# Chunked attention, SoLU and leaky MLP on one core: the scores of a tile taken three tiles ahead, behind the values' product

## The chip, the cores and the metric

The kernel runs on one core of a Trainium2 chip. The metric is the device time of one execution in microseconds (us), lower is better. The median over three runs is compared; besides, one execution was profiled, and every duration below is from that one.

## What is computed

```
# q, k, v: (8, 8, 576, 64); heads cut into chunks of 64 positions
scores = scale * q_c @ k_c.T ; scores -= max(scores)
attn   = exp(scores) / (sum(exp(scores)) + 1e-9)
x      = (attn @ v_c), heads laid side by side   # (4608, 512)

h    = x @ w_in                                  # (4608, 1024)
solu = h * softmax(h)
ln   = (solu - mean) / sqrt(var + 1e-6) * g_ln
y    = ln @ w_out                                # (4608, 512)

h2  = y @ w_in2 ; g = max(0.01 * h2, h2)         # (4608, 2048)
out = g @ w_out2                                 # (4608, 512)
```

The weights arrive as 64-bit floats and are made 32-bit on the chip. The large products are taken in split form (a high part and a remainder), three matmuls for one.

## The kernel before

The 4608 rows are 36 tiles of 128 (`T = 36`). The program has a first part, up to about 560 us, in which the loop `for t in range(T + 2)` (L506) makes attention, the first product, SoLU, the norm and the second product, and a second part (L622, L665) with the last two products. The change is in the first part alone. Everything stands in an order written out by hand, under `manual_schedule`: each engine gets its instructions in the order in which the Python code records them, and waits where an input is not there yet.

One tile goes through the loop in a staggered way. In iteration t, these steps are recorded (names as in the code, then what the trace calls the results):

- `qk_mm` (L287, `s_ps`): the scores of tile t+2, 8 small matmuls into one PSUM bank. Its inputs `qt` and `kbd` come by `load_qk`, from SyncE's queue.
- `solu_a(t-1)`: on VectorE (DVE) the maximum of h, 1024 wide (L374, `z`), then on ScalarE (ACT) the exponential of h (L376, `us`).
- `softmax_a(t+2)`: on DVE the maximum of the scores (L298, `st`) and a subtraction (L300, `es`), then the exponential on ACT (L303, `es`).
- `take_magnitudes` (L93), `convert` (L101 to L109, DVE) and `finish` (L116, L117 or L167 on ACT, L118 or L168 on GpSimd (POOL), for `w_in2` also L164 and L165 on DVE): pieces of the weights. Two pieces at once in iterations 0, 1 and 6 to 11, one in the others up to 33.
- `ff1_mm(t, 0)` and `ff1_mm(t, 1)` (L359, `h_ps`): the first product, two halves of 12 matmuls. The first half needs `xs` of tile t.
- `solu_b(t-1)` (L381, `us`): on DVE the product of h and its exponential. It needs the result of L376.
- `pt_mm`, `pt_copy` (L320, L326, `pt`), `softmax_b(t+2)` (L307 to L310), `pv_mm(t+1)` (L337, `x_ps`): the transposed weights of the attention and the values' product, in 64x64 pieces.
- `x_split(t+1)`: a copy on ACT (L348) and a subtraction on DVE (L349), both `xs`.
- `lnT_mm(t-2)`, `lnT_split` (L414, L420 on ACT, L421 on DVE, `lnT`), and `y1_group` (L430, `y_ps`, 24 matmuls), copied out by ACT (L438, `ys`).

From iteration 5 on there is a y group in each iteration. In every fourth (5, 9, 13, ...; `late`) the y group stands behind the values' product and needs the `lnT` of tile t-2, in the others ahead of it. Up to iteration 4 there is none, and TensorE has the scores right behind the values' product there already, since nothing else stands at the end of an iteration.

Of the kernel before, what the change touches and what calls it, by code (L numbers as in the profile page):

```python
# [23 lines left out]
T = NT // P  # L24
# [19 lines left out]
def kernel(  # L44
# [22 lines left out]
    def bank(tag, name):  # L67
        return (ps2 if tag == "ef" else ps1).tile([P, 512], F32, tag=tag, name=name)
# [113 lines left out]
    def take_magnitudes(n=1):  # L182
        for _ in range(min(n, len(loaded))):
            end, raw = loaded.pop(0)
            begun.append((end, raw, magnitudes(raw)))
# [18 lines left out]
    def y_load(g):  # L204
        if g < NG:
            for name, r, c in (("a11", 0, 0), ("a21", 1, 0), ("a22", 1, 1), ("a12", 0, 1)):
                yr[name] = yp.tile([P, 2, TH], F32, tag=name, name=name)
                sync.dma_start(
                    out=yr[name], in_=y_d[g][:, 2 * c : 2 * c + 2, r * TH : (r + 1) * TH]
                )  # L210
# [31 lines left out]
    def w_load():  # L242
        at = next(w_order, None)
        if at:
            w = ws.tile([P, 2, 2 * P], F32R, tag="w", name="w_s")
            sync.dma_start(out=w.bitcast(F32), in_=wi_d[at[0]][:, w_place[at[1]]])
            w_tiles.append(w)

    wf_bufs = None
    with tc.manual_schedule():  # L250

        with ExitStack() as phase:
# [12 lines left out]
            def load_qk(t):  # L265
                if t >= T:
                    return
                qt[t] = pa.tile([P, KD, P], F32, tag="qt", name="qt")
                sync.dma_start(out=qt[t], in_=q[t])
                kb = kbd[t % 2]  # L270
                for e in range(2):
                    sync.dma_start(out=kb[e * D : (e + 1) * D, e], in_=k[t, e * D : (e + 1) * D])

            def load_v(t):
                if t >= T:
                    return
                vt[t] = pa.tile([P, KD, 2, D], F32, tag="vt", name="vt")
                sync.dma_start(out=vt[t], in_=v[t])
# [3 lines left out]
            def qk_mm(t):  # L282
                ps = s_ps[t] = bank("ef" if t in (1, 2) else "s", "s_ps").rearrange("p (h n) -> p h n", h=H)
                kb, qq = kbd[t % 2], qt.pop(t)
                for i in range(KD):
                    for c in range(2):
                        pe.matmul(  # L287
                            ps[c * D : (c + 1) * D, 2 * i : 2 * i + 2, :],
                            lhsT=qq[:, i, c * D : (c + 1) * D],
                            rhs=kb[:, :, i, c, :],  # L290
                            start=True,
                            stop=True,
                        )

            def softmax_a(t):
                ps = s_ps.pop(t)
                sm = st8[t] = pa.tile([P, 2, H], F32, tag="st8", name="st8")
                dve.reduce_max(sm[:, 0, :], ps, axis=AX)  # L298
                e = es[t] = pa.tile([P, H, D], F32, tag="es", name="es")
                dve.tensor_tensor(  # L300
                    e, ps, sm[:, 0, :].unsqueeze(2).to_broadcast([P, H, D]), op=ALU.subtract
                )
                act.activation(e, e, AF.Exp, scale=scale)  # L303
# [26 lines left out]
            def pv_mm(t):  # L330
                ps = x_ps[t] = bank("ptx", "x_ps").rearrange("p (i n) -> p i n", i=KD)
                vv, pp = vt.pop(t), pt.pop(t)
                for i in range(KD):
                    for c in range(2):
                        for e in range(2):
                            r = slice(e * D, (e + 1) * D)
                            pe.matmul(  # L337
                                ps[r, i, c * D : (c + 1) * D],
                                lhsT=vv[r, i, c, :],
                                rhs=pp[r, i, c * D : (c + 1) * D],  # L340
                                start=True,
                                stop=True,
                            )

            def x_split(t):
                ps = x_ps.pop(t)
                x = xs[t] = pa.tile([P, 2, KD, P], F32R, tag="xs", name="xs")
                act.activation(x[:, 0], ps, AF.Copy)  # L348
                dve.tensor_tensor(x[:, 1], ps, x[:, 0].bitcast(F32), op=ALU.subtract)  # L349
# [21 lines left out]
            def solu_a(t):  # L371
                h = hs[t].rearrange("p n f -> p (n f)")
                z = sol[t] = wk.tile([P, 8], F32, tag="z", bufs=3, name="z")
                dve.reduce_max(z[:, 0:1], h, axis=AX, negate=True)  # L374
                u = us[t] = wk.tile([P, FF1], F32, tag="us", bufs=3, name="us")
                act.activation(u, h, AF.Exp, bias=z[:, 0:1], accum_out=z[:, 1:2])  # L376
# [46 lines left out]
            def y1_group(b, m):  # L423
# [21 lines left out]
                g, o = divmod(pair, 3)  # L445
                sync.dma_start(out=y_d[g][:, m, o * 256 : o * 256 + 512 - at], in_=ys[:, at:])


            start = ExitStack()
            stage = start.enter_context(tc.tile_pool(name="start", bufs=5))  # L450
# [55 lines left out]
            for t in range(T + 2):  # L506
                if t == T:
                    att.close()
                    yp = ctx.enter_context(
                        tc.tile_pool(name="yp", bufs=1, side="right", reuse_waits="tile")  # L510
                    )
                    ws = ctx.enter_context(
                        tc.tile_pool(name="ws", bufs=WS, side="right", reuse_waits="tile")
                    )
                    y_load(0)
                    for _ in range(WS):
                        w_load()
                load_qk(t + 3)
                load_v(t + 2)
                b, g = divmod(t - 5, 4)  # L520
                groups = [(b, g)] if 5 <= t < T else []
                if t == T - 1:
                    groups = []
                elif t == T:
                    groups = [(NB - 2, 2), (NB - 2, 3)]
                elif t == T + 1:
                    groups = [(NB - 1, m) for m in range(KD)]
                late = g == 0 or t == T - 1
                pieces = 0 if t >= T - 2 else 2 if t < 2 or 6 <= t < 12 else 1
                if 0 < t < T - 2:  # L530
                    qk_mm(t + 2)
                if 1 <= t <= T:
                    solu_a(t - 1)
                if t + 2 < T:
                    softmax_a(t + 2)
                take_magnitudes(pieces)
                if t < T:
                    ff1_mm(t, 0)
                if 1 <= t <= T:
                    solu_b(t - 1)  # L540
                if t + 1 < T:
                    pt_mm(t + 1)
                if t + 2 < T:
                    softmax_b(t + 2)
                convert(pieces)
                if t + 1 < T:
                    pt_copy(t + 1)
                if late and t >= 2:
                    lnT_mm(t - 2)
                    lnT_split(t - 2, 0)  # L550
                    lnT_split(t - 2, 1)
                if 1 <= t <= T:
                    solu_c(t - 1)
                    solu_d(t - 1)
                if t == T:
                    for _, do in Y_STEPS:
                        do(0)
                if groups and not late:
                    for bm in groups:
                        y1_group(*bm)  # L560
                    if t + 1 < T:
                        pv_mm(t + 1)
                        x_split(t + 1)
                    if t >= 2:
                        lnT_mm(t - 2)
                        lnT_split(t - 2, 0)
                        lnT_split(t - 2, 1)
                    if t < T:
                        ff1_mm(t, 1)
                    finish(pieces)  # L570
                else:
                    if t >= 2 and not late:
                        lnT_mm(t - 2)
                        lnT_split(t - 2, 0)
                        lnT_split(t - 2, 1)
                    if t < T:
                        ff1_mm(t, 1)
                    if t + 1 < T:
                        pv_mm(t + 1)
                        x_split(t + 1)  # L580
                    finish(pieces)
                    for bm in groups:
                        y1_group(*bm)
# [171 lines left out]
```

## Time and profile before

| what | value |
|---|---|
| median of three runs (lowest, highest) | 1338.85 us (1338.63, 1339.13) |
| profiled execution, whole | 1339.17 us |
| its span from first to last instruction | 1337.4 us |
| TensorE (PE) busy | 1292.0 us, 97% |
| DVE, ACT, POOL busy | 608.4, 530.0, 448.1 us |
| mean granted TensorE clock | 0.994 |

Busy time is counted over the whole span. The engines other than TensorE are much busier in the first 230 us than later, so the shares say little on a single stage; the rows below are taken by stage.

### The profile page before, as it was taken

The numbers are of one execution on the slowest core, as the hardware profiler recorded it, in microseconds if no ns is written. First come the engines' busy times: TensorE is split into PE (matmuls) and PEld (weight loads), VectorE is DVE, ScalarE is ACT, GpSimd is POOL, SyncE is SP. The second block draws the span as 40 slices with busy tenths as digits, with TensorE's granted clock in tenths as the row PEclk, the third lists the DMA queues.
The fourth block names the chain that finished last, engine by engine and source line by source line (L and its number), as shares of the span: only waits on it lengthen the run. The fifth ranks groups of instructions, "written<-read, shape, count | busy, mean of one in ns | idle before, by whom it ended". The sixth has DMA issues, their size and how long they took to land.

```text
span 1337.4 us, 20370 instructions
## 1 busy us (share of the span) xinstructions
PE 1292.0 (97%) x7632; PEld 1116.0 (83%) x7632; DVE 608.4 (45%) x1030; ACT 530.0 (40%) x953; POOL 448.1 (34%) x488
## 2 busy tenths in 40 slices
PE   3799999999999999899999999999999999999998
PEld 3678788788888888689989998999899989989997
DVE  7988887766666654511232233222412331232112
ACT  3665554444444443423333324333332333333322
POOL 3556765433433431212222222222222222222222
PEclk9999999999999999899999999999999999999999
DMA  7345776544444432257645544554554455445441
GB/s 244 116 130 190 255 245 195 173 163 136 144 141 156 128 103 73 102 212 229 196 134 165 166 118 129 150 170 119 159 163 121 118 165 165 119 117 166 118 118 48
DMA packets 100608, 202.66 MB, mean 152 GB/s; under 512 B 10784, under 2 KB 28192, under 8 KB 98080
## 3 DMA queue, kind: packets, MB, share of 16 engines
q1 hardware_dynamic: 100512, 201.37, 49.1%
q8 instruction: 61, 1.00, 0.3%
q14 instruction: 35, 0.29, 0.1%
HBM read 159.39 MB, written 41.94 MB: 151 GB/s over the span
## 4 chain that ended last, share of the span: by engine, by line
PE 86%; DVE 8%; ACT 2%; DMA 1%; issue 1%; SPq 0%; POOL 0%; ACTq 0%; DVEq 0%
PE o_ps L665 28%; PE h_ps L622 25%; PE y_ps L430 14%; PE h_ps L359 12%; PE x_ps L337 2%; PE s_ps L287 2%; PE ln_ps L414 2%; PE pt_ps L320 1%; DVE yo L228 1%; DVE wf L109 1%; DVE wf L105 1%; ACT yo L227 1%; DVE wf L103 1%; DMA raw<-in_w_in 1%; DVE us L381 1%
## 5 line engine op out<-in xcount | busy, mean ns | idle before, releaser
L665 PE MATMUL o_ps<-wo_s,g 128*128 128x512 f32 x1728 | 447.4, 390 | 0.0
L622 PE MATMUL h_ps<-yo,w_s 128*128 128x384 f32 x2016 | 407.4, 337 | 3.0 <-DVE c L633 3.0
L604 POOL TENSOR_TENSOR g<-t,g 128x384 fp32r<-128x384 f32 x192 | 194.7, 1014 | 583.0 <-ACT g L603 496.8
L622 PEld LDWEIGHTS h_ps<-yo,w_s 128*128 128x128 f32 x2016 | 362.4, 188 | 32.8 <-DVE c L633 5.1
L665 PEld LDWEIGHTS o_ps<-wo_s,g 128*128 128x128 f32 x1728 | 319.9, 188 | 41.7
L359 PE MATMUL h_ps<-wi,xs 128*128 128x512 f32 x864 | 220.3, 403 | 2.7 <-DVE xs L349 2.7
L430 PE MATMUL y_ps<-lnT,wo 128*128 128x512 f32 x864 | 208.6, 398 | 6.5 <-DVE lnT L421 6.5
L430 PEld LDWEIGHTS y_ps<-lnT,wo 128*128 128x128 f32 x864 | 162.4, 191 | 40.9 <-DVE lnT L421 4.7
L633 DVE TENSOR_TENSOR u<-h_ps,p 128x384 f32<-128x384 f32 x96 | 53.5, 557 | 312.3 <-PE h_ps L622 304.4
L359 PEld LDWEIGHTS h_ps<-wi,xs 128*128 128x128 f32 x864 | 158.5, 190 | 41.5 <-issue 6.0
L601 ACT ACTIVATE t<-c 128x384 f32<-128x384 f32 x144 | 75.7, 526 | 286.8 <-DVE c L633 286.7
L633 DVE TENSOR_TENSOR c<-h_ps,u 128x384 f32<-128x384 f32 x96 | 53.5, 557 | 125.1 <-PE h_ps L622 73.0
L603 ACT ACTIVATE g<-t 128x384 fp32r<-128x384 f32 x192 | 100.8, 525 | 6.0
L310 POOL TENSOR_TENSOR es<-es,st 128x512 f32<-128x512 f32 x36 | 37.6, 1046 | 179.9 <-DVE st L309 152.5
L601 ACT ACTIVATE t<-h_ps 128x384 f32<-128x384 f32 x48 | 23.6, 492 | 186.8 <-PE h_ps L622 186.8
L438 ACT ACTIVATE ys<-y_ps 128x512 f32<-128x512 f32 x36 | 21.4, 596 | 133.7 <-PE y_ps L430 133.6
L376 ACT ACTIVATE us<-h_ps,z 128x1024 f32<-128x1024 f32 x36 | 40.1, 1115 | 55.8 <-DVE z L374 55.7
L349 DVE TENSOR_TENSOR xs<-x_ps,xs 128x512 fp32r<-128x512 f32 x36 | 24.8, 688 | 74.3 <-ACT xs L348 74.3
L633 DVE TENSOR_TENSOR c<-h_ps,p 128x384 f32<-128x384 f32 x48 | 26.7, 556 | 66.4 <-PE h_ps L622 66.4
L374 DVE TENSOR_REDUCE z<-h_ps 128x1 f32<-128x1024 f32 x36 | 43.8, 1217 | 22.2 <-PE h_ps L359 22.2
L287 PE MATMUL s_ps<-kbd,qt 128*64 128x128 f32 x576 | 42.0, 291 | 10.5 <-DMA kbd<-in_k 10.4
L287 PEld LDWEIGHTS s_ps<-kbd,qt 128*64 128x64 f32 x576 | 33.0, 144 | 21.3 <-issue 20.6
(68 smaller groups left out, 1138.8 us busy)
## 6 DMA issues: line engine op xcount, KB each, us to landing
w_s<-wi_d SPq DMA_DIRECT2D x336, 256.0 KB, 2.7
wi_d<-wi SPq DMA_DIRECT2D x8, 1792.0 KB, 6.7
raw<-in_w_out SPq DMA_DIRECT2D x24, 512.0 KB, 4.1
raw<-in_w_in SPq DMA_DIRECT2D x18, 512.0 KB, 6.0
qt<-in_q SPq DMA_DIRECT2D x36, 256.0 KB, 4.9
kbd<-in_k SPq DMA_DIRECT2D x72, 128.0 KB, 4.9
vt<-in_v SPq DMA_DIRECT2D x36, 256.0 KB, 4.2
a<-y_d SPq DMA_DIRECT2D x24, 384.0 KB, 5.8
```

The lines of the kernel that those rows point to most:

```text
L287: pe.matmul(ps[c * D : (c + 1) * D, 2 * i : 2 * i + 2, :], lhsT=qq[:, i, c * D : (c + 1) * D], rhs=kb[:, :, i, c, :], start=True, stop=True,)
L310: pool.tensor_tensor(e, e, sm[:, 1, :].unsqueeze(2).to_broadcast([P, H, D]), op=ALU.mult)
L359: pe.matmul(h[:, n, :], lhsT=x[:, a, kk, :], rhs=w[:, b, kk % 2, n, :], start=(kk == 0 and a == 0 and b == 0), stop=(kk == KD - 1 and a == 1),
L374: dve.reduce_max(z[:, 0:1], h, axis=AX, negate=True)
L376: act.activation(u, h, AF.Exp, bias=z[:, 0:1], accum_out=z[:, 1:2])
L430: pe.matmul(ps, lhsT=w[:, a, kk % 4, m * P : (m + 1) * P], rhs=lnT[:, c, kk, pairs, :], start=(kk == 0 and a == 0 and c == 0), stop=(kk == ...
L601: act.activation(t, src, AF.Prelu, alpha=0.01)
L603: act.activation(g[:, 0], t, AF.Copy)
L604: pool.tensor_tensor(g[:, 1], t, g[:, 0].bitcast(F32), op=ALU.subtract)
L622: pe.matmul(ps, lhsT=w[:, a, kk * P : (kk + 1) * P], rhs=y[:, c, kk, :], start=(first and kk == 0 and a == 0 and c == 0), stop=(kk == 1 an ...
L633: dve.tensor_tensor(o, ps, x, op=ALU.add)
L665: pe.matmul(ps, lhsT=x[:, a, i * P : (i + 1) * P], rhs=wos[j][:, h, c, :], start=(j == 0 and h == 0 and a == 0 and c == 0), stop=(j == QUA ...
```

## The change

The scores of a tile are recorded one iteration earlier: `qk_mm(t + 3)` directly behind `pv_mm(t + 1)`, and `softmax_a(t + 3)` directly behind `x_split(t + 1)`. `load_qk` moves to the same place and reaches one tile further. The number of instructions and the buffers stay as they are.

```diff
+            def attend(t):
+                pv_mm(t + 1)
+                if t + 3 < T:
+                    qk_mm(t + 3)
+                    load_qk(t + 4)
+                x_split(t + 1)
+                if t + 3 < T:
+                    softmax_a(t + 3)
...
-                load_qk(t + 3)
+                if t == 0:
+                    load_qk(3)
                 load_v(t + 2)
...
-                if 0 < t < T - 2:
-                    qk_mm(t + 2)
                 if 1 <= t <= T:
                     solu_a(t - 1)
-                if t + 2 < T:
-                    softmax_a(t + 2)
+                if t == 0:
+                    softmax_a(2)
...
                     if t + 1 < T:
-                        pv_mm(t + 1)
-                        x_split(t + 1)
+                        attend(t)
```

The last hunk stands twice, once in each branch of the order of the y group.

On TensorE, an iteration with the y group ahead (from the values' product on) reads before:

```order
L337 MATMUL x_ps<-pt,vt 64x64 x16
L414 MATMUL ln_ps<-ident,us 128x128 x8
L359 MATMUL h_ps<-wi_244,xs 128x512 x12
L287 MATMUL s_ps<-kbd_107,qt 64x128 x8
L359 MATMUL h_ps<-wi_180,xs 128x512 x12
L320 MATMUL pt_ps<-ident,es 128x128 x4
L430 MATMUL y_ps<-lnT,wo_355 128x512 x12
```

and of the change:

```order
L337 MATMUL x_ps<-pt,vt 64x64 x16
L287 MATMUL s_ps<-kbd_107,qt 64x128 x8
L414 MATMUL ln_ps<-ident,us 128x128 x8
L359 MATMUL h_ps<-wi_244,xs 128x512 x12
L359 MATMUL h_ps<-wi_180,xs 128x512 x12
L320 MATMUL pt_ps<-ident,es 128x128 x4
L430 MATMUL y_ps<-lnT,wo_373 128x512 x12
```

The 8 matmuls of the scores have moved from between the two halves of the first product to behind the values' product; the halves now stand side by side.

On ACT, one of the iterations 2 to 4 (with one piece of `w_out1`, L116 and L117) reads before, from the copy of `lnT` on:

```order
L420 ACTIVATE lnT<-ln_ps 128x4x128 x2
L348 ACTIVATE xs<-x_ps 128x512
L116 ACTIVATE wf<-wf,g_sb 128x512
L117 ACTIVATE wo_588<-wf 128x512
L376 ACTIVATE us,z<-h_ps,z 128x1024
L303 ACTIVATE es<-es 128x512
L93 ACTIVATE wf<-raw 128x512
```

and of the change:

```order
L420 ACTIVATE lnT<-ln_ps 128x4x128 x2
L348 ACTIVATE xs<-x_ps 128x512
L303 ACTIVATE es<-es 128x512
L116 ACTIVATE wf<-wf,g_sb 128x512
L117 ACTIVATE wo_606<-wf 128x512
L376 ACTIVATE us,z<-h_ps,z 128x1024
L93 ACTIVATE wf<-raw 128x512
```

The exponential of the scores (L303) has moved from behind that of h (L376) to ahead of the two weight copies. On DVE, an iteration from 6 on whose y group stands ahead, and in which a pair of `w_in2` pieces is finished, reads before:

```order
L349 TENSOR_TENSOR xs<-x_ps,xs 128x512
L421 TENSOR_TENSOR lnT<-ln_ps,lnT 128x4x128 x2
L164 TENSOR_TENSOR wc<-wf,wc 128x256
L165 TENSOR_TENSOR wc<-wf,wc 128x256
L374 TENSOR_REDUCE z<-h_ps 128x1
L298 TENSOR_REDUCE st_1149<-s_ps 128x8
L300 TENSOR_TENSOR es<-s_ps,st_1149 128x512
L381 SCALAR_TENSOR_TENSOR us,z<-h_ps,us 128x1024
```

and of the change:

```order
L349 TENSOR_TENSOR xs<-x_ps,xs 128x512
L298 TENSOR_REDUCE st_1104<-s_ps 128x8
L300 TENSOR_TENSOR es<-s_ps,st_1104 128x512
L421 TENSOR_TENSOR lnT<-ln_ps,lnT 128x4x128 x2
L164 TENSOR_TENSOR wc<-wf,wc 128x256
L165 TENSOR_TENSOR wc<-wf,wc 128x256
L374 TENSOR_REDUCE z<-h_ps 128x1
L381 SCALAR_TENSOR_TENSOR us,z<-h_ps,us 128x1024
```

The two steps on the scores have left the place between the maximum of h (L374) and the product that needs the exponential of h (L381). In iterations up to 4 the same two rows move from there to directly behind L349, with nothing between them and L374.

## Rows read from the trace of the kernel before

**Rows 1.** The page, busy us of each engine, share of the span, instructions.

```profile
PE 1292.0 (97%) x7632; PEld 1116.0 (83%) x7632; DVE 608.4 (45%) x1030; ACT 530.0 (40%) x953; POOL 448.1 (34%) x488
```

**Rows 2.** Windows, one iteration each: length, busy us of the engines, clock, DMA share, GB/s.

```profile
core 0: us, PE busy (x) PEld busy (x) DVE busy (x) ACT busy (x) POOL busy (x), PEclk, DMA share, GB/s
82.79:92.67 9.88, 9.41 (x86) 7.48 (x85) 9.61 (x19) 6.94 (x13) 5.69 (x8) 1.00 0.43 134
...
153.18:173.68 20.50, 18.33 (x113) 14.53 (x113) 16.36 (x29) 7.78 (x13) 14.54 (x16) 0.92 0.84 260
...
306.85:321.59 14.74, 14.74 (x110) 11.94 (x109) 9.79 (x18) 6.92 (x12) 5.72 (x8) 1.00 0.44 143
```

**Rows 3.** Timeline of TensorE at three places: start, duration, line, out<-in.

```profile
43.24 1.15 PE L337 MATMUL x_ps<-pt,vt 64*64 64x64 f32 x32
44.32 1.09 PE L287 MATMUL s_ps<-kbd,qt 128*64 128x128 f32 x16
...
48.22 0.60 PE L320 MATMUL pt_ps<-ident,es 128*128 128x128 f32 x4
...
323.51 3.01 PE L359 MATMUL h_ps<-wi,xs 128*128 128x512 f32 x12
326.45 1.09 PE L287 MATMUL s_ps<-kbd,qt 128*64 128x128 f32 x16
327.48 3.02 PE L359 MATMUL h_ps<-wi,xs 128*128 128x512 f32 x12
330.33 0.38 PE L320 MATMUL pt_ps<-ident,es 128*128 128x128 f32 x2
...
528.95 5.73 PE L359 MATMUL h_ps<-wi,xs 128*128 128x512 f32 x24
534.52 1.03 PE L414 MATMUL ln_ps<-ident,us 128*128 128x128 f32 x8
```

**Rows 4.** Timeline of DVE, iterations 2 and 3, from one xs to the next.

```profile
75.94 0.68 DVE L349 TENSOR_TENSOR xs<-x_ps,xs 128x512 fp32r<-128x512 f32 x1
76.54 1.21 DVE L374 TENSOR_REDUCE z<-h_ps 128x1 f32<-128x1024 f32 x1
77.67 0.68 DVE L298 TENSOR_REDUCE st<-s_ps 128x8 f32<-128x512 f32 x1
78.38 0.69 DVE L300 TENSOR_TENSOR es<-s_ps,st 128x512 f32<-128x512 f32 x1
79.03 1.23 DVE L381 SCALAR_TENSOR_TENSOR us<-h_ps,us 128x1024 f32<-128x1024 f32 x1
...
85.82 0.68 DVE L349 TENSOR_TENSOR xs<-x_ps,xs 128x512 fp32r<-128x512 f32 x1
```

**Rows 5.** Timeline of ACT; in brackets the idle time and what ended it.

```profile
50.84 0.66 ACT L93 ACTIVATE wf<-raw 128x512 f32<-128x512 f32 x1 [1.03 <-DMA raw<-in_w_out]
51.41 0.58 ACT L326 ACTIVATE pt<-pt_ps 128x512 f32<-128x512 f32 x1
...
74.86 0.72 ACT L116 ACTIVATE wf<-wf,g_sb 128x512 f32<-128x512 f32 x1 [0.16 <-DVE wf L109]
75.61 0.63 ACT L117 ACTIVATE wo<-wf 128x512 fp32r<-128x512 f32 x1
77.79 1.11 ACT L376 ACTIVATE us<-h_ps,z 128x1024 f32<-128x1024 f32 x1 [1.54 <-DVE z L374]
...
79.17 0.63 ACT L303 ACTIVATE es<-es 128x512 f32<-128x512 f32 x1 [0.18 <-DVE es L300]
```

**Rows 6.** Timeline of TensorE, the y groups of iterations 5 and 9.

```profile
95.24 5.74 PE L430 MATMUL y_ps<-lnT,wo 128*128 128x512 f32 x24 [1.42 <-DVE lnT L421]
...
156.50 6.69 PE L430 MATMUL y_ps<-lnT,wo 128*128 128x512 f32 x21 [2.17 <-DVE lnT L421]
```

**Rows 7.** Timeline of DVE, iterations 7 and 8 (two weight pieces each).

```profile
127.35 0.69 DVE L349 TENSOR_TENSOR xs<-x_ps,xs 128x512 fp32r<-128x512 f32 x1 [0.97 <-ACT xs L348]
...
133.82 1.22 DVE L381 SCALAR_TENSOR_TENSOR us<-h_ps,us 128x1024 f32<-128x1024 f32 x1
...
142.09 0.69 DVE L349 TENSOR_TENSOR xs<-x_ps,xs 128x512 fp32r<-128x512 f32 x1 [0.97 <-ACT xs L348]
```

More of the change, by code (lines that the diff above doesn't have):

```diff
@@ L578 @@
                     if t + 1 < T:
-                        pv_mm(t + 1)
-                        x_split(t + 1)
+                        attend(t)
                     finish(pieces)
```

## The prediction

> **What bounds the kernel now.** I read the page first, then the windows by iteration, then the timelines of TensorE, DVE and ACT. Over the span TensorE is busy 97% [rows 1], so whatever TensorE saves or waits shows in the time. The windows show that the first part of the loop is another case [rows 2]: in the iteration from 82.79 to 92.67 DVE is busy 9.61 of 9.88 us, and TensorE 9.41, partly stretched by waiting inside its blocks. In the iteration from 306.85 TensorE is busy all of its 14.74 us and DVE 9.79. So up to iteration 5 DVE sets the pace, later TensorE does, and in between, with two weight pieces an iteration, the two are close: DVE idles only 0.97 us ahead of its xs [rows 7]. Two y groups wait for DVE's lnT, 1.42 and 2.17 us [rows 6].
>
> **What TensorE saves.** Between the halves of the first product stand the scores. From the first half to the transposes it is 330.33 - 323.51 = 6.82 us [rows 3]. Where 24 of these matmuls stand in one run, it takes 534.52 - 528.95 = 5.57 us, and the scores take 327.48 - 326.45 = 1.03. Behind the values' product they cost no more: in iteration 0 they start there 44.32 - 43.24 = 1.08 us after it started, and take 1.09 like the others. So 6.82 - 5.57 - 1.03 = 0.22 us is saved per iteration, in the 28 iterations 5 to 32 (I take it for the late ones too, an estimate): 6.2 us if nothing waits. Below iteration 5 TensorE's order doesn't change.
>
> **What DVE loses up to iteration 5.** Before, DVE takes the maximum of h (76.54), then 1.36 us of work on the scores (77.67, 78.38), then L381 at 79.03 [rows 4]. In that gap ACT makes the exponential of h: it starts at 77.79 [rows 5], and L381 follows 1.24 us later with no idle time. The scores' work is exactly what fills the gap. In the change it stands ahead of the maximum; the gap of 1.25 us stays and is empty.
>
> ACT makes it worse. The scores' exponential (L303) now stands ahead of the copies L116 and L117, and must wait for DVE's L300. Counted from the start X of DVE's xs: L298 starts at X + 0.60, L300 ends at X + 2.0 (0.60, and 1.40 from 77.67 to 79.07, [rows 4]), L303 starts at X + 2.1 (79.07 to 79.17, [rows 5]), L116 0.54 later, L117 0.75 after that, L376 about 0.55 later at X + 3.95, and L381 at X + 5.2. Before it started at X + 3.1. So an iteration with one piece gets 2.1 us longer, and nothing else is slack: from L381 to the next xs DVE has 85.82 - 79.03 = 6.79 us of solid work. In iterations 0 and 1, two pieces put two more copies (1.3 us) ahead of L376: about 3.4, less 0.3 that such copies held L376 up before (an estimate); I take 3.1. Iterations 0 to 4: 2 x 3.1 + 3 x 2.1 = **+12.5 us** until lnT, and with it the y group of iteration 5 (95.24), comes. TensorE has no cover for that; it waits in the first product and ahead of this y. Only the scores, which now precede this y group, fill 1.0 us of the wait: -1.0.
>
> All this rests on ACT keeping its order. The trace shows it: at 50.84 ACT sits idle 1.03 us for a weight's transfer although the transposes (48.22 to 48.82) have been ready for the copy that comes next (51.41) [rows 3, 5]. The Trainium skill, "TensorE: Matmul & The Clock Gate" (engine queue depth, in the table at its head), calls the queues of ScalarE, VectorE and GpSimd strictly first in, first out; if a ready copy could pass a waiting exponential, the second rival's sum would hold instead.
>
> **Iterations 6 to 9.** From xs to L381 it is 133.82 - 127.35 = 6.47 us before, without idle time [rows 7]. After, two holes open: lnT's copies on ACT stand behind L303, so DVE waits from X + 2.0 to about X + 3.3 (0.1, L303's 0.54, one copy of 0.55 like that at 51.41, and 0.1), and the gap ahead of L381, 1.3 with nothing in it. That is 2.6; I take 2.7. What hides it is 0.97 us of idle time an iteration [rows 7]. Iteration 6 starts with TensorE ahead (DVE idles there after the long y); then the holes of 6, 7 and 8 less two idles reach the lnT of iteration 9: 3 x 2.7 - 2 x 1.0 = **+6.1**. Its y group, which waits 2.17 us already, starts so much later, and again takes the scores into its wait: -1.0. Iterations 10 to 13 go the same way: two with two pieces, one with one (some 1.7 us less to convert), and a y group at 13 that did not wait. Worked through like 6 to 9, that leaves +2.8 and, with the scores in the wait, -1.0.
>
> **From 14 to 32** DVE has room [rows 2]. 19 x 0.22 = 4.2 us are saved. In the four late ones among them lnT comes about 0.4 us after the scores end (the xs-to-L381 stretch is longer, as above): +1.8 in all.
>
> **TensorE's clock.** In the iteration with the 2.17 us wait the granted clock is 0.92 over 20.50 us [rows 2, 6]: 1.6 us lost at the lower level, 1.2 GHz. Iterations 5 and 13 now get waits of about 2.5 us, each worth 0 or 1.6. I count one, 1.6.
>
> SyncE's queue: `load_qk` is issued in the place of the values' product and has a whole iteration until its scores, as before; it moves ahead of the stores of `w_in2`, no later. I cost it at nothing; covered by an iteration of 9.9 us at least.
>
> **The sum**, against the profiled execution's 1339.17 us: 12.5 - 1.0 + 6.1 - 1.0 + 2.8 - 1.0 - 4.2 + 1.8 + 1.6 = +17.6; my chain of starts, done with the rows to two places, gives 0.3 to 0.5 less (the first matmul behind a y group is better fed), so +17.1: 1356.3. The median lies 0.3 lower: **1356 us**.
>
> **Rivals.** *Only TensorE's saving counts* (faster): if DVE and ACT had room everywhere, 6.2 us come off: 1332.6. For it speaks TensorE's 97%; against it DVE's 9.61 of 9.88. It decides once the holes on DVE are below the 0.3 us of slack in such an iteration; I find 2.1. The Trainium skill, "TensorEngine Tiling (Array Packing)", key properties, says that a change of the tiling mode drains the engine; the 64-wide products would then change mode three times an iteration instead of four, and this rival is what that rule would make of the change. The trace agrees as far as 0.22 us goes. Chance 8%. *The hole without the queue* (about no change): ACT's copies don't hold L376 up and lnT isn't late. Then 5 x 1.25 - 1.0 + 3 x 1.3 - 2 x 1.0 - 1.0 - 4.2 = +2.0: 1341. It needs ACT out of order, which 50.84 speaks against, or a slack that I overlook. Chance 10%. *The clock falls with every wait* (slower still): TensorE now waits 2.6 to 3.6 us in each of iterations 1 to 4 as well, and if the lower clock reaches DVE's chain through a late xs, up to 1.6 us come on top at three or four places: +5, 1361. Against it: after xs TensorE has about 3 us to spare before DVE needs the next. Chance 12%.
>
> **How the numbers follow.** Forecast 70%, by itself 1350 to 1360: the piece terms of iterations 6 to 13 are good to 4 us, the clock to 2. The range 1341 to 1361 takes in the second rival's time and leaves out the first, half of the second and half of the third (19%). Within 0.2% (2.7 us, about what a measurement of this kernel can tell from no change) falls most of the second rival. Faster 0.09, same 0.07, slower 0.84.
>
> **What would show it.** In the changed profile: DVE idle ahead of L381, released by ACT's L376, 1.3 to 3.3 us in iterations 1 to 4; ACT idle ahead of L303, released by DVE, with L116 behind it; TensorE waiting at L359 for DVE's xs 2.5 us and more where it was about 0.5; the y of iteration 5 near 107.7 and that of 9 near 174; the first product in runs of 24 in 5.57 us from iteration 6 on. Wrong would be: no idle time ahead of L381, or L116 ahead of L303 in time, or the y of iteration 5 below 100.

## The result, and the profile after

| | before | change |
|---|---|---|
| median (lowest to highest) | 1338.94 us (1338.63 to 1339.13) | 1357.56 us (1356.95 to 1357.75) |
| ratio, 95% interval | | 1.0139 (1.0121 to 1.0156): slower |
| span of the profiled execution | 1337.4 us | 1355.9 us |

The forecast was 1356 us. The page has TensorE 3.3 us busier, and DVE and ACT no busier at all:

```profile
PE 1295.3 (96%) x7632; PEld 1124.8 (83%) x7632; DVE 605.9 (45%) x1030; ACT 526.3 (39%) x953; POOL 449.1 (33%) x488
```

So of the 18.5 us of span, 15.2 are idle time of TensorE: it waits 8.1 us in the first product for xs (2.7 before), 11.2 at the y groups for lnT (6.5) and 5.5 ahead of the values' product (1.6). The 3.3 us of busy time are net: the y groups take 212.7 us instead of 208.6 and the first product 215.5 instead of 220.3, at a mean granted clock of 0.987 (0.994 before). The timeline of DVE from one xs to the next shows where the waits come from (in brackets the idle time and what ended it). Counted by the values' products, [rows 4] run from the xs of iteration 3 to that of iteration 4; these rows stand one iteration earlier and have the same steps:

```profile
71.15 0.69 DVE L109 SCALAR_TENSOR_TENSOR wf<-raw,wf 128x512 uint32<-128x512 uint32 x1
...
72.95 0.68 DVE L349 TENSOR_TENSOR xs<-x_ps,xs 128x512 fp32r<-128x512 f32 x1
73.55 0.68 DVE L298 TENSOR_REDUCE st<-s_ps 128x8 f32<-128x512 f32 x1
74.27 0.69 DVE L300 TENSOR_TENSOR es<-s_ps,st 128x512 f32<-128x512 f32 x1
74.88 1.22 DVE L374 TENSOR_REDUCE z<-h_ps 128x1 f32<-128x1024 f32 x1
78.08 1.23 DVE L381 SCALAR_TENSOR_TENSOR us<-h_ps,us 128x1024 f32<-128x1024 f32 x1 [1.99 <-ACT us L376]
...
84.86 0.68 DVE L349 TENSOR_TENSOR xs<-x_ps,xs 128x512 fp32r<-128x512 f32 x1
```

Between the maximum of h (L374) and the product L381 there is now a hole of 1.99 us. From xs to xs it is 84.86 - 72.95 = 11.91 us (and the same in the next iteration, the one of [rows 4]), where it was 9.88 [rows 4]; from L381 to the next xs it is 6.78, as before. ACT's timeline in the same stretch says why the hole is longer than the exponential of h:

```profile
69.74 0.59 ACT L348 ACTIVATE xs<-x_ps 128x512 fp32r<-128x512 f32 x1
75.05 0.63 ACT L303 ACTIVATE es<-es 128x512 f32<-128x512 f32 x1 [4.72 <-DVE es L300]
75.59 0.70 ACT L116 ACTIVATE wf<-wf,g_sb 128x512 f32<-128x512 f32 x1
76.33 0.63 ACT L117 ACTIVATE wo<-wf 128x512 fp32r<-128x512 f32 x1
76.86 1.10 ACT L376 ACTIVATE us<-h_ps,z 128x1024 f32<-128x1024 f32 x1
```

ACT is idle for 4.72 us ahead of the scores' exponential (L303). The two weight copies, whose input DVE had made by 71.84 (L109 above), stand behind it until 75.59, and only then comes L376. In the iterations with a pair of weight pieces, DVE shows both of the holes that were forecast there, one ahead of L421 and one ahead of L381 (against [rows 7]):

```profile
141.38 0.68 DVE L349 TENSOR_TENSOR xs<-x_ps,xs 128x512 fp32r<-128x512 f32 x1
141.98 0.68 DVE L298 TENSOR_REDUCE st<-s_ps 128x8 f32<-128x512 f32 x1
142.69 0.69 DVE L300 TENSOR_TENSOR es<-s_ps,st 128x512 f32<-128x512 f32 x1
144.56 1.29 DVE L421 TENSOR_TENSOR lnT<-ln_ps,lnT 128x512 fp32r<-128x512 f32 x2 [1.18 <-ACT lnT L420]
...
150.46 1.23 DVE L381 SCALAR_TENSOR_TENSOR us<-h_ps,us 128x1024 f32<-128x1024 f32 x1 [1.27 <-ACT us L376]
```

xs to L381 takes 9.08 us instead of 6.47. TensorE's timeline has the y groups of iterations 5, 9 and 13, the first two to be read against [rows 6]:

```profile
108.21 5.51 PE L430 MATMUL y_ps<-lnT,wo 128*128 128x512 f32 x23 [0.82 <-DVE lnT L421]
...
174.67 8.56 PE L430 MATMUL y_ps<-lnT,wo 128*128 128x512 f32 x24 [4.12 <-DVE lnT L421]
...
237.82 7.36 PE L430 MATMUL y_ps<-lnT,wo 128*128 128x512 f32 x24 [2.16 <-DVE lnT L421]
```

The third, and the values' product of iteration 34, were before at

```profile
217.15 5.75 PE L430 MATMUL y_ps<-lnT,wo 128*128 128x512 f32 x24
...
527.02 1.15 PE L337 MATMUL x_ps<-pt,vt 64*64 64x64 f32 x32
```

The y groups start 13.0 us (95.24), 18.2 us (156.50) and 20.7 us (217.15) later than before. After that the kernel wins back: the values' product of iteration 34 now starts at 544.87, 17.9 us later. What it wins on TensorE, in an iteration with the y group ahead [rows 3]:

```profile
326.91 1.15 PE L337 MATMUL x_ps<-pt,vt 64*64 64x64 f32 x32
327.99 1.09 PE L287 MATMUL s_ps<-kbd,qt 128*64 128x128 f32 x16
329.01 1.09 PE L414 MATMUL ln_ps<-ident,us 128*128 128x128 f32 x8
329.86 5.70 PE L359 MATMUL h_ps<-wi,xs 128*128 128x512 f32 x24
335.40 0.60 PE L320 MATMUL pt_ps<-ident,es 128*128 128x128 f32 x4
```

The two halves run as one in 335.40 - 329.86 = 5.54 us. The windows of one iteration each follow (length, busy us of the engines, granted clock, DMA share, GB/s), to be read against [rows 2]:

```profile
core 0: us, PE busy (x) PEld busy (x) DVE busy (x) ACT busy (x) POOL busy (x), PEclk, DMA share, GB/s
...
68.28:81.41 13.13, 11.02 (x86) 8.83 (x85) 10.76 (x23) 7.95 (x16) 6.18 (x8) 0.87 0.35 102
...
168.37:191.81 23.44, 19.32 (x112) 15.49 (x113) 17.23 (x36) 9.47 (x17) 14.47 (x16) 0.85 0.71 258
...
326.91:341.42 14.51, 14.51 (x110) 12.02 (x109) 9.82 (x18) 6.81 (x12) 5.71 (x8) 1.00 0.46 146
```

An iteration late in the loop takes 14.51 us, not 14.74. In the early ones DVE is no longer solidly busy (10.76 of 13.13 us), and the granted clock is below 1 in several.

### The profile page after: what moved, and what is told of

Same layout as the page of the kernel before. It is cut to its first block, busy times and chain, and to the rows that moved or that the text cites. A ratio compares the mean times of both kernels' runs of the same rounds, so it can differ in the third digit from the quotient of the medians.

```text
span 1355.9 us, 20337 instructions
## 1 busy us (share of the span) xinstructions
PE 1295.3 (96%) x7632; PEld 1124.8 (83%) x7632; DVE 605.9 (45%) x1030; ACT 526.3 (39%) x953; POOL 449.1 (33%) x488
## 4 chain that ended last, share of the span: by engine, by line
PE 78%; DVE 13%; ACT 4%; issue 2%; DMA 2%; POOL 0%; SPq 0%; ACTq 0%; DVEq 0%
PE o_ps L672 27%; PE h_ps L629 25%; PE y_ps L430 13%; PE h_ps L359 8%; PE x_ps L337 2%; DVE lnT L421 2%; DVE us L381 1%; PE ln_ps L414 1%; DVE wf L103 1%; DVE wf L105 1%; DVE wf L109 1%; PE s_ps L287 1%; DVE yo L228 1%; ACT us L376 1%; DMA raw<-in_w_in 1%
## 5 line engine op out<-in xcount | busy, mean ns | idle before, releaser
L430 PE MATMUL y_ps<-lnT,wo 128*128 128x512 f32 x864 | 212.7, 403 | 11.6 <-DVE lnT L421 11.2
L359 PE MATMUL h_ps<-wi,xs 128*128 128x512 f32 x864 | 215.5, 402 | 8.4 <-DVE xs L349 8.1
L359 PEld LDWEIGHTS h_ps<-wi,xs 128*128 128x128 f32 x864 | 162.0, 192 | 43.8 <-DVE xs L349 9.9
L381 DVE SCALAR_TENSOR_TENSOR us<-h_ps,us 128x1024 f32<-128x1024 f32 x36 | 44.1, 1225 | 77.5 <-ACT us L376 77.5
L303 ACT ACTIVATE es<-es 128x512 f32<-128x512 f32 x36 | 22.8, 632 | 109.4 <-DVE es L300 109.4
L118 POOL TENSOR_TENSOR wo<-wf,wo 128x512 fp32r<-128x512 f32 x24 | 30.9, 1287 | 87.0 <-ACT wo L117 87.0
L421 DVE TENSOR_TENSOR lnT<-ln_ps,lnT 128x512 fp32r<-128x512 f32 x72 | 46.1, 684 | 25.7 <-ACT lnT L420 25.7
L337 PEld LDWEIGHTS x_ps<-pt,vt 64*64 64x64 f32 x1152 | 37.2, 137 | 18.5 <-issue 10.4
```

The lines of the kernel that those rows point to most:

```text
L337: pe.matmul(ps[r, i, c * D : (c + 1) * D], lhsT=vv[r, i, c, :], rhs=pp[r, i, c * D : (c + 1) * D], start=True, stop=True,)
L359: pe.matmul(h[:, n, :], lhsT=x[:, a, kk, :], rhs=w[:, b, kk % 2, n, :], start=(kk == 0 and a == 0 and b == 0), stop=(kk == KD - 1 and a == 1),
L381: dve.scalar_tensor_tensor(u, h, 1.0, u, op0=ALU.mult, op1=ALU.mult, accum_out=z[:, 2:3])
L421: dve.tensor_tensor(dst[:, 1], ps, dst[:, 0].bitcast(F32), op=ALU.subtract)
L430: pe.matmul(ps, lhsT=w[:, a, kk % 4, m * P : (m + 1) * P], rhs=lnT[:, c, kk, pairs, :], start=(kk == 0 and a == 0 and c == 0), stop=(kk == ...
```

## The experiments

Two causes were to be told apart, and each from other things that the change moves: the order on DVE and ACT (my theory), and the matmuls, their PSUM bank and the loads (the rival). Each version below is the changed kernel with the edit shown; `early(t)` says in which iterations the softmax steps go out early. Where the steps are not early they stand where they were before, one iteration later.

**1. Only the scores' matmuls and loads moved.**

```diff
-                if t + 3 < T:
+                if t + 3 < T and early(t):      # early: never
                     softmax_a(t + 3)
...
-                if t == 0:
+                if t + 2 < T and (t == 0 or not early(t - 1)):
                     softmax_a(t + 2)
```

> The scores' matmuls stand behind the values' product as in the change, but the softmax steps (L298, L300, L303) stay where they were, one iteration later. Theory (holes on DVE and the queue on ACT): both are gone, TensorE's saving is left, 26 x 0.22 us, and in iterations 5 and 9 the scores fill 1.1 us of a wait each: 1338.9 - 7.9 = 1331 (1329 to 1334), the y group of iteration 5 again at 95.2 us. Rival (the matmuls' new place, the longer held scores bank or the moved loads cost the time): as slow as the change, about 1357.

Measured: 1331.54 us, ratio to the kernel before 0.9954 (0.9942 to 0.9967). It is faster than both kernels, by 0.5% and 1.8%. DVE fills the gap again; from its timeline:

```profile
77.01 1.22 DVE L374 TENSOR_REDUCE z<-h_ps 128x1 f32<-128x1024 f32 x1
78.14 0.68 DVE L298 TENSOR_REDUCE st<-s_ps 128x8 f32<-128x512 f32 x1
78.86 0.69 DVE L300 TENSOR_TENSOR es<-s_ps,st 128x512 f32<-128x512 f32 x1
79.49 1.22 DVE L381 SCALAR_TENSOR_TENSOR us<-h_ps,us 128x1024 f32<-128x1024 f32 x1
```

and TensorE's y groups of iterations 5 and 9 stand within half a microsecond of where they were (95.24 and 156.50):

```profile
95.71 2.57 PE L430 MATMUL y_ps<-lnT,wo 128*128 128x512 f32 x10 [0.36 <-DVE lnT L421]
...
156.50 5.74 PE L430 MATMUL y_ps<-lnT,wo 128*128 128x512 f32 x24 [2.62 <-DVE lnT L421]
```

The whole loss of the change, and more, hangs on the softmax steps. The rival falls: neither the matmuls' new place nor the bank nor the moved loads cost anything that shows in the time.

**2. The DVE steps early, the exponential late.**

```diff
 def softmax_a(t):
...
-    act.activation(e, e, AF.Exp, scale=scale)
+def softmax_e(t):      # called behind solu_a(t - 1), for tile t + 2
+    act.activation(es[t], es[t], AF.Exp, scale=scale)
```

> The change, with the scores' exponential on ACT (L303) put back behind that of h (L376), and the two DVE steps left in their new place. Theory: ACT's weight copies no longer wait, only the gap of 1.25 us ahead of L381 stays: iterations 0 and 1 lose 1.0 to 1.1, iterations 2 to 4 lose 1.4 each, 6.3 until the y group of iteration 5 (at 101.5), 1 to 2 more up to 9, against 5 to 7 us saved by TensorE: 1340 (1337 to 1343). Rival (the gap on DVE alone makes the loss, the exponential's place on ACT is of no account): about 1357.

Measured: 1338.41 us, ratio 0.9998 (0.9989 to 1.0006). In this kernel the lines are two further down (L383 is L381 above, L378 is L376). DVE still has the gap, but only that:

```profile
91.93 1.21 DVE L376 TENSOR_REDUCE z<-h_ps 128x1 f32<-128x1024 f32 x1
94.47 1.23 DVE L383 SCALAR_TENSOR_TENSOR us<-h_ps,us 128x1024 f32<-128x1024 f32 x1 [1.33 <-ACT us L378]
```

and on ACT the copies are done long before:

```profile
88.92 0.72 ACT L116 ACTIVATE wf<-wf,g_sb 128x512 f32<-128x512 f32 x1 [1.47 <-DVE wf L109]
89.68 0.63 ACT L117 ACTIVATE wo<-wf 128x512 fp32r<-128x512 f32 x1
93.23 1.11 ACT L378 ACTIVATE us<-h_ps,z 128x1024 f32<-128x1024 f32 x1 [2.93 <-DVE z L376]
```

The y group of iteration 5, on TensorE:

```profile
100.81 0.50 PE L432 MATMUL y_ps<-lnT,wo 128*128 128x512 f32 x1 [1.77 <-DVE lnT L423]
```

So, taken off in this order, the empty gap costs the ratio 0.0044 (0.9998 - 0.9954), 5.9 us; the exponential's place in ACT's queue the other 0.0141, 18.9 us. Each is good to some 2 us, by the intervals. Up to the y group of iteration 5 it is 5.9 and 6.0 us, counted from DVE's xs of iteration 0, which the three kernels reach at different times (experiment 1: 95.71 - 45.54 = 50.17; here 100.81 - 44.78 = 56.03; the change 108.21 - 46.16 = 62.05). The rival that the gap alone does it falls.

**3 to 5. The loss by stage.** The softmax steps early in iterations 0 to 4 alone, in 5 to 13 alone, and from 14 on alone:

```diff
 def early(t):
-    return False
+    return t <= 4          # 3;   4: 5 <= t <= 13;   5: t >= 14
```

> The softmax steps early in iterations 0 to 4 alone, late as before from 5 on; the scores' matmuls early throughout. Theory: the loss of the first stage alone, 13 us, on top of the version with all softmax steps late: 1344 (1342 to 1346), the y group of iteration 5 near 108. Rival (the loss sits in iterations 5 to 13, where two weight pieces are converted): under 1335.

> The softmax steps early in iterations 5 to 13 alone. Theory: the other part of the loss, 1357.5 - 1331 - 13 - 1.5 = 12 us on top of the version with all of them late: 1343 (1340 to 1345); the y group of iteration 9 waits 4 us or more. Rival (the losses don't add, since the late start of one stage hides the other's): 1349 or more, or under 1337.

> The softmax steps early in iterations 14 to 32 alone, where DVE has room. Theory: only the y groups of iterations 17, 21, 25 and 29 start some 0.3 to 0.6 us late: 1331.5 + 1.5 = 1333 (1331.5 to 1334). Rival (what the stages 0 to 4 and 5 to 13 leave open of the 26 us, 3.3 us, sits here too): 1335.

| softmax steps early in | median | ratio (95%) | above experiment 1 |
|---|---|---|---|
| 0 to 4 | 1345.06 us | 1.0054 (1.0038 to 1.0069) | 0.0100: 13.4 us |
| 5 to 13 | 1340.76 us | 1.0022 (1.0012 to 1.0031) | 0.0068: 9.1 us |
| 14 to 32 | 1334.57 us | 0.9963 (0.9951 to 0.9976) | 0.0009: 1.2 us |
| all (the change) | 1357.56 us | 1.0139 (1.0121 to 1.0156) | 0.0185: 24.8 us |

The parts add up to 23.7 us, within the intervals of the whole; the runs show no sign that the stages hide one another. The first and the second came as expected. The third came out above its range (1331.5 to 1334) and near its rival's 1335, but its runs lie between 1331.71 and 1336.21 and its interval overlaps that of experiment 1, so the times settle neither. In its trace four y groups wait 0.42, 0.26, 0.25 and 0.26 us, 1.2 us in all, which experiment 1 doesn't have. From TensorE's timeline, the y group of iteration 5 in the first of the three:

```profile
106.54 5.76 PE L430 MATMUL y_ps<-lnT,wo 128*128 128x512 f32 x24 [2.38 <-DVE lnT L421]
```

and that of iteration 9 in the second:

```profile
161.73 8.52 PE L430 MATMUL y_ps<-lnT,wo 128*128 128x512 f32 x24 [4.12 <-DVE lnT L421]
```

**6. What saves on TensorE.** As experiment 1, with the scores one block further, behind the norm's transposes, in the 21 iterations with the y group ahead:

```diff
     attend(t)              # without the scores
     if t >= 2:
         lnT_mm(t - 2)
+        if t + 3 < T:
+            qk_mm(t + 3)
+            load_qk(t + 4)
```

> As the version with only the scores' matmuls moved, but in the 21 iterations whose y group stands ahead the scores stand behind the norm's transposes (L414) instead of directly behind the values' product; the two halves of the first product stay side by side. Theory (the saving comes from the halves being one run, not from the scores being next to the values' product): within 0.7 us of 1331.5, and the halves again at 5.54 us. Rival (each change between 128-wide and 64-wide products costs a drain of about 0.1 to 0.2 us, and here there is one more of them): 2 to 4 us slower, 1333.5 to 1335.5.

Measured: 1334.54 us, ratio 0.9967 (0.9954 to 0.9979), 1.7 us above experiment 1 by the ratios, whose intervals overlap. The trace decides for the single iteration. TensorE's timeline:

```profile
288.20 1.15 PE L337 MATMUL x_ps<-pt,vt 64*64 64x64 f32 x32
289.28 1.09 PE L414 MATMUL ln_ps<-ident,us 128*128 128x128 f32 x8
290.30 1.09 PE L287 MATMUL s_ps<-kbd,qt 128*64 128x128 f32 x16
291.32 5.74 PE L359 MATMUL h_ps<-wi,xs 128*128 128x512 f32 x24
296.90 0.60 PE L320 MATMUL pt_ps<-ident,es 128*128 128x128 f32 x4
...
302.90 0.27 PE L337 MATMUL x_ps<-pt,vt 64*64 64x64 f32 x2
```

The halves are one run here too (5.58 us), yet the iteration takes 302.90 - 288.20 = 14.70 us, nearly the 14.74 of before. The transposes now take 1.02 us to the start of the scores, where they take 0.85 to that of the first product in the change (329.86 - 329.01).

The starts of the single matmuls in the traces of experiments 1 and 6 say more. From the last transpose to the scores it is 0.20 us, against 0.11 between transposes. From the last pair of the values' product it is 0.15 us, to the scores (64x64 to 128x64) as well as to the transposes (64x64 to 128x128), against 0.06 between its pairs. So each of these changes of the products' shape costs about 0.09 us; so does that from the y group to the values' product (0.32 against 0.23). From the last transpose to the first product, where the shape stays, it is 0.03 us, 0.17 less than to the scores. An iteration with the y group ahead has four such changes in the kernel before and in this one, and three in the change and in experiment 1.

My theory that the joined halves save falls but for the 0.04 us from 14.74 to 14.70, and the rival holds: 21 x 0.19 = 4 us of the span at most. The two profiled executions are 3.6 us apart (1332.5 and 1328.9), but the runs of experiment 1 alone spread as far (1330.67 to 1334.28).

**7. The loads at their old place.**

```diff
-                    load_qk(t + 4)      # behind the scores
...
+                load_qk(t + 3)          # at the head of the iteration
```

> As the version with only the scores' matmuls moved, but the loads of queries and keys go out at the head of an iteration as before, half an iteration ahead of the scores instead of a whole one. Theory (their move costs nothing and gains little, since a load lands some 5 us after its issue): 1331.5 to 1334, with a wait for the keys in a few early iterations, where stores and weight loads stand in front. Rival (the move of the loads is half of what makes the gain): above 1335, with TensorE waiting for the keys in most iterations.

Measured: 1373.46 us, ratio 1.0258 (1.0244 to 1.0272); in time the rival holds, by far. TensorE waits 39.8 us for the keys in all, against 9.8 in experiment 1. But it doesn't wait in most iterations, as the rival had it: of the nine waits seven, of 2.84 to 5.87 us, stand between 130 and 297 us. They make 29.5 of the some 41 us; the rest was not taken apart, and the mean granted clock is 0.982 here, 0.994 in experiment 1. One of the seven, on TensorE:

```profile
130.18 1.97 PE L287 MATMUL s_ps<-kbd,qt 128*64 128x128 f32 x16 [4.38 <-DMA kbd<-in_k]
```

and on SyncE's queue:

```profile
120.73 0.33 SPq L169 DMA_DIRECT2D wi_d<-wi  x1
121.16 0.38 SPq L269 DMA_DIRECT2D qt<-in_q  x1
121.59 2.33 SPq L272 DMA_DIRECT2D kbd<-in_k  x2
```

The loads stand behind the store of `w_in2` (1792 KB), which waits for POOL. The keys are issued at 121.59 and TensorE starts on them at 130.18, 8.6 us later, where the median landing is 4.5 in this run. The scores of this tile are wanted in the same iteration, behind the values' product, and come too early for that; in the change the same loads go out ahead of that store (the keys at 125.58, the store at 135.45).

## Why the prediction was right

Its mechanism held step by step, and its terms came out as follows.

- **DVE up to iteration 5**, +12.5 us: 13.0 at the y group (108.21 against 95.24), 13.4 by experiment 3. From xs to xs, the two iterations with two pieces got 3.05 and 3.02 us longer (3.1 forecast) and the three with one 2.03 each (2.1): 12.15 us. Of the 2.03, the gap was taken as 1.25 us and is 1.33, and the queue on ACT was taken as 0.85 and is 0.70. ACT does keep its order: copies that were ready stood 3.75 us (71.84 to 75.59) behind a waiting exponential. The other 0.82 us came ahead of the xs of iteration 0 (46.16 against 45.34), where both kernels have the same instructions; the granted clock of that stretch was 0.82 (25.70 to 44.34) against 0.90 before. No term of the sum had it.
- **Iterations 6 to 9**, +6.1 and -1.0: from the y group of 5 to that of 9 it grew by 18.2 - 13.0 = 5.2 us (5.1 forecast). The holes of 1.3 and 1.3 us are 1.18 and 1.27.
- **Iterations 10 to 13**, +2.8 and -1.0, with the clock +0 to 1.6: 20.7 - 18.2 = 2.5. The y group of 13 waits 2.16 us; 2.5 was forecast.
- **From 14 on**, -1.0 - 4.2 + 1.8, with the clock up to +1.6: 17.9 - 20.7 = -2.8. The late y groups wait 1.2 us together, not 1.8.
- **The clock**, one drop of 1.6 us counted: it was mis-sized. The y group of 9, at 1.6 us over its usual time before (7.31 to the next block), is at 2.8 now (8.40, where 5.6 is undisturbed), and that of 13 takes 7.20: 1.2 + 1.6 us more than before. The 1.2 are offset by terms that came out smaller. The last y groups of the first part took another 0.6 us more (24.02 us from 574.99 to the start of the second part, where it was 23.39), again with the same instructions in both kernels. In the stretches that begin with the values' products of iterations 1, 2 and 4 the clock fell as well (0.88, 0.87 and 0.87), which the third rival had at 12%; there it stayed off DVE's chain, as the slack of some 3 us said. Of the two waits that the forecast weighed, that of iteration 5 came out at 0.82 us, not 2.5, and left the clock at 1.00.
- **TensorE's saving**, 0.22 us an iteration: 14.74 - 14.51 = 0.23. The size was right, the reason was not shown by the rows that I priced it from: experiment 6 puts 0.19 of it on one change of shape fewer and the rest on the joined halves. The Trainium skill, "TensorEngine Tiling (Array Packing)", key properties, which I had set under the first rival, says that changing the tiling mode drains the engine. The trace agrees: each change of shape lengthens the step between two matmuls by about 0.09 us, that from 64x64 to 128x64 included. That it is a drain which takes the time, the trace doesn't show.
- **The loads** at nothing: right for the change. But experiment 7 shows that their move is needed for it, not a mere by-product; I had given them no price in case they stayed.

The 0.8 us in iteration 0 and the 0.6 us at the last y groups, which no term had, make up the difference between the 17.1 us of the sum and the 18.5 us of the span. That the other terms agree so closely in the end is in part luck: 0.35 us less on DVE, 0.5 less in iterations 10 to 13 and 1.0 less from 14 on stand against the 1.2 us more of clock at the y group of 9.

The first rival's time, 1332.6, is near that of experiment 1 (1331.5): it is what the same move gives once the softmax steps stay where they were. The second rival, the gap without the queue, 1341, is what experiment 2 makes (1338.4).

## What to carry to other kernels

Moving a producer's matmuls is one edit, moving the work that consumes them is another; the second can undo the first. Before moving a step on an in-order engine, look at what it stands between: short work between a reduction and the product that waits for another engine's result was filling a hole that the shares of busy time never showed. And a step that waits must not go in front of ready ones: one exponential, a few rows earlier in ACT's order, cost three times what the emptied gap did (18.9 and 5.9 us).

## What the runs showed of the hardware that was not expected

Waits of the same length ended at different clocks. The y group of iteration 9 waits 2.62 us both in experiment 1 and in experiment 2. In the first it then runs undisturbed (5.74 us, the row above) at a granted clock of 1.00 over the iteration; in the second it takes 8.56, with a clock of 0.84:

```profile
161.59 8.56 PE L432 MATMUL y_ps<-lnT,wo 128*128 128x512 f32 x24 [2.62 <-DVE lnT L423]
```

What TensorE did ahead of it was the same: from the values' product of iteration 8 to this y group it is 17.45 us in both (139.05 to 156.50 and 144.14 to 161.59), with the same blocks at the same distances. So a wait of this size is worth 0 to 2.8 us on top of itself, and neither its length nor the blocks just ahead of it tell which. What decides it stays open.
